# The first layer of a gated feed-forward block by seven products of halves, with its weights streamed from a scratch buffer in HBM

## The chip, the cores and the metric

The kernel runs on one core of a Trainium2 chip. The metric is the device time of one execution in microseconds (us); lower is better. A core has a matrix engine (PE in the profile; its weight loads have a row of their own, PEld), a vector engine (DVE), a scalar engine (ACT), a general engine (POOL), a queue processor that issues the transfers (SP), and 16 DMA engines between HBM and the on-chip memory SBUF. PE writes its results to eight PSUM banks of 128 x 512 float32, and DVE and ACT read them from there. Each engine works through its own instructions in the order in which they were written and waits on semaphores for the others.

## The reference

Eight batches with eight heads of attention: 512 local queries per head see 32 global keys and a window of 32 keys to each side; 32 global queries see everything. The 4608 rows that come out (512 features) go through a normalised, gated feed-forward block:

```python
rms = np.sqrt(np.mean(x * x, axis=-1, keepdims=True) + 1e-06)
xn = x / rms * rms_g
g = xn @ w_gate                         # 512 -> 1536
silu = g * (1.0 / (1.0 + np.exp(-g)))
val = xn @ w_val                        # 512 -> 1536
return (silu * val @ w_out).astype(np.float32)   # 1536 -> 512
```

## The kernel before

**Number format.** Every large product is done in float16 with operands split in a high and a low half: a product a*b is three matmuls, high*high, high*low and low*high, added up in float32 in PSUM. The weights are split and scaled on the chip at the start.

**Chunks.** The rows go through the block in nine chunks. Chunks 0 to 7 are the 512 local rows of one batch each; chunk 8 is the 256 global rows of all batches. Features lie on the partitions (four k-blocks of 128), rows on the free axis.

**First layer** (`moe_in`, L954 to L959, called by `moe_f`). The 1536 columns of each weight matrix are taken as 12 blocks f of 128. For each f and each of the two matrices (w = 0 gate, w = 1 value) 4 k-blocks x 3 matmuls of 128x128 weights by 512 rows add up in one PSUM bank, "pg" for the gate and "pv" for the value: 288 matmuls a chunk. Then ACT takes the tanh of the gate bank (L969), DVE makes the gated value from tanh and bank (L970) and multiplies it by the value bank (L977), ACT rounds to float16 (L980) and POOL takes the low half (L151, through the helper `sub`). All the split weights stay in SBUF, in 12 buffers "wf".

**Second layer** (`moe_block`, L1014). Four blocks of 128 rows, each 12 f x 3 matmuls of 512 columns into a "po" bank; ACT or DVE scales the result into SBUF (L1025, L1027) and SP stores it (L1028): 144 matmuls a chunk.

**Order.** Chunk 0 and the preparation of the weights follow a list written out by hand (`ORDER`); its letters name steps, for instance `N1`, `D1`, `U1`, `H1`, `Y1` for the norm of chunk 1 and `O`, `o` for the second layer of chunk 0. From chunk 1 on, each chunk is a list of 72 work items (48 of six first-layer matmuls, 24 of six second-layer matmuls). After each item `slot` issues those steps of the next chunk's attention that are due: loads L and V, scores S (L648), least value M and exponentials (L599, L610), division D (POOL, L625), turning T (DVE, L630), values A and B (L691), taking over X and Y (DVE, L704), and for the global queries GL, GS (L762), GM, GN, GT (L805), GA (L819), GD, GX. Each step has a least distance in items from the step that it needs. At items 56 to 66 the next chunk's norm follows, and `norm_split` (L946, L949, L149/L151) makes its four high and low operand tiles "xh" and "xl". Chunks 2 to 7 have two local attention units of four heads and, from gplan, one or two global units.

All transfers are issued on SP's queue, in order.

Of the kernel before, what the change touches and what calls it, by code (L numbers as in the profile page):

```python
# [22 lines left out]
P = 128  # L23
# [7 lines left out]
NGH = NG // 2  # L31
GC = 112
# [33 lines left out]
def attention_moe_kernel(  # L66
# [23 lines left out]
    LG = (4, 7)  # L90
# [6 lines left out]
    pool = ctx.enter_context(tc.tile_pool(name="pool", bufs=2))  # L97
    psum = ctx.enter_context(tc.tile_pool(name="psum", bufs=2, space=bass.MemoryType.PSUM))
# [92 lines left out]
    def gain_scale():  # L191
        power(gp[0], 1, 11, gs[:, 0:1])
# [114 lines left out]
    def group(g, fs):  # L307
# [22 lines left out]
        def powers():  # L330
            s = pool.tile([P, 2], F32, tag="ws", bufs=7, name=f"ws{g}")[:, :n]
            for j, f in enumerate(fs):
                scale[f] = s[:, j : j + 1]
            power(st["ps"], n, 15, s)
# [83 lines left out]
    job.update(K0=out_sum, K1=out_total, K2=out_scale)  # L418


    def local_unit(c, hp):
# [109 lines left out]
        def divide():  # L531
            assert len(xt) == hp
            xt.append(pool.tile([P, 512], F32, tag="x", bufs=4, name=f"x{c}_{hp}"))
# [31 lines left out]
    def local_halves(c, b, hp, xt):  # L565
# [25 lines left out]
        def softmax(x, bk, gs):  # L591
# [5 lines left out]
            for g in gs:  # L597
# [10 lines left out]
                )  # L608
            for g in gs:
# [90 lines left out]
        def take(z):  # L700
            x = pool.tile([P, 512], F32, tag="x", bufs=4, name=f"x{c}_{2 * hp + z}")
            xt.append(x)
            for half in range(2):
                nc.vector.tensor_copy(  # L704
                    x[:, half * 256 : (half + 1) * 256], st["a"][2 * z + half][:, :256]
                )
# [9 lines left out]
            ("S", scores, 1, [("L", LG[0]), ("^Y", 1)]),  # L716
        ]
        for j, (x, bk) in enumerate(((0, 0), (1, 0), (0, 1), (1, 1))):
            steps += [
                (f"M{j}", lambda x=x, bk=bk: softmax(x, bk, (0, 1)), 0, [("S", 2 * j + 1)]),  # L720
                (f"N{j}", lambda x=x, bk=bk: softmax(x, bk, (2, 3)), 0, [(f"M{j}", 1)]),
                (f"D{j}", lambda x=x, bk=bk: divide(x, bk), 0, [(f"N{j}", 2)]),
# [3 lines left out]
            ("A", lambda: values(blocks[:SPLIT]), 1, [("T3", 1), ("V", 4)]),  # L726
# [6 lines left out]
    def global_unit(b):  # L733
# [3 lines left out]
        def load():  # L737
# [5 lines left out]
            v = []  # L743
            for i in range(3):
                t = pool.tile([P, 1152], F32, tag="st", bufs=ST, name=f"gv{b}{i}")
                n = min(1024, 5 * 512 - i * 1024)
                nc.sync.dma_start(t[:GC, :n], gv[b, :, i * 1024 : i * 1024 + n])
                v += [t[:, j * 512 : (j + 1) * 512] for j in range(n // 512)]
            st.update(kq=kq, v=v)
# [88 lines left out]
        def turn():  # L838
# [8 lines left out]
            ("GS", scores, 1, [("GL", GG[0])]),  # L847
            ("GM", lambda: softmax(0), 0, [("GS", 1)]),
# [79 lines left out]
    def norm_all(ch, c, n):  # L928
# [3 lines left out]
        ps = attn_bank(f"ss{c}")  # L932
# [20 lines left out]


    def moe_in(ch, w, f, n, ps, ks):
        for k in ks:
            o = (w * NK + k) * P
            for i, (a, z) in enumerate(((0, "xh"), (0, "xl"), (1, "xh"))):
                nc.tensor.matmul(  # L959
                    ps[:, :n],  # L960
                    wf[f][:, a, o : o + P],
# [5 lines left out]
    def moe_gate(f, n, pg):  # L967
        t = pool.tile([P, 512], F32, tag="t", bufs=3, name=f"t{f}")
        nc.scalar.activation(t[:, :n], pg[:, :n], AF.Tanh, scale=half_inv[:, f : f + 1])  # L969
        nc.vector.scalar_tensor_tensor(t[:, :n], t[:, :n], 1.0, pg[:, :n], ALU.add, ALU.mult)  # L970
        return t

    def moe_h(ch, f, n, t, pv, on):
        if f % 2 == 0:
            ch["h"] = pool.tile([P, 2, 2, 512], F16, tag="h", bufs=NF // 2, name=f"h{f}")
        h = ch["h", f] = ch["h"][:, f % 2]
        nc.vector.scalar_tensor_tensor(  # L977
            t[:, :n], t[:, :n], c_h[:, f : f + 1], pv[:, :n], ALU.mult, ALU.mult
        )
        nc.scalar.copy(h[:, 0, :n], t[:, :n])  # L980
        sub(on, h[:, 1, :n], t[:, :n], h[:, 0, :n])

    def moe_f(ch, f, n, on):
        ps = {}

        def half(w, i):
            if i == 0:
                ps[w] = psum.tile(
                    [P, 512], F32, tag="pg" if w == 0 else "pv", bufs=1, name=f"p{w}_{f}"
                )  # L990
            moe_in(ch, w, f, n, ps[w], range(2 * i, 2 * i + 2))

        def gate():
            ps["t"] = moe_gate(f, n, ps[0])

        def inner():
            moe_h(ch, f, n, ps["t"], ps[1], on)
# [112 lines left out]
    for c in range(NCH):  # L1110
# [3 lines left out]
        for i, un in enumerate(units):  # L1114
# [6 lines left out]
            for name, fn, pe, after in steps:  # L1121
                st = {"name": name, "fn": fn, "pe": pe, "c": c, "x": xi, "after": [], "at": None}
                st["from"] = UNIT[len(units)][i]
# [16 lines left out]
    def ready(st):  # L1140
        if st["c"] > 0 and clock[0] < base.get(st["c"] - 1, 1 << 30) + st["from"]:
            return False
# [29 lines left out]
    first_chunk()  # L1172
    eng = mybir.EngineType
# [4 lines left out]
    assert not job, list(job)  # L1178
    row = SL
    for c in range(1, NCH):  # L1180
        n = width[c]
        ch = chunks[c]
        base.setdefault(c, clock[0])
        work = [w for f in range(NF) for w in moe_f(ch, f, n, "P")]
        work += [w for j in range(n // P) for w in moe_block(ch, j, row)]
        norm_at = NORM[0]
        last = c + 1 == B
        at = {}
        if c + 1 < NCH:
# [3 lines left out]
            at[NORM[1]] = lambda c=c, nx=nx: norm_sums(chunks[c + 1], c + 1, nx)  # L1193
            at[NORM[2]] = lambda c=c, nx=nx: norm_all(chunks[c + 1], c + 1, nx)
            at[NORM[3]] = lambda c=c, nx=nx: norm_split(chunks[c + 1], c + 1, nx)
        for k, (products, rest) in enumerate(work):
            products()
            if c + 1 < NCH:
                slot(1 if k < norm_at - 6 else 2, c + 1 if k < min(norm_at, SECOND) else c + 2)
                if k == norm_at - 1:  # L1200
                    while chunks[c + 1]["left"]:
                        slot(2, c + 1)
# [4 lines left out]
            if rest:  # L1207
                rest()
        row += n
# [126 lines left out]
```

## Time and profile before

| | |
|---|---|
| median of three runs | 981.94 us (979.61 to 983.16) |
| the profiled execution | 978.9 us, span of its instructions 977.1 us |
| PE, DVE, ACT, POOL busy | 939.2, 451.0, 409.2, 194.4 us |
| moved by the transfers issued in the kernel | 86.46 MB |
| one chunk of 512 rows in the steady part (280.89 to 389.62) | 108.73 us |

The span runs from the first to the last instruction; the 1.8 us between it and the profiled execution's own time lie around it. A busy PE is not a PE at its peak: matmuls are pipelined, each is shown with the time from its start to its end (379 ns for 512 columns) while the next starts 216 ns later. So the pace of a stretch of matmuls is read from its length and its count. In the groups by line a row gives the line, the engine, the operation, the names, the shapes and the count, then busy microseconds and the mean nanoseconds of one, then the idle time before it. The windows view gives one stretch in each row: its length, then for each engine the busy time and the count, the granted TensorE clock, the share of DMA time and the rate.

### The profile page before, as it was taken

Reading aid. Unit: us, or ns where it says so; the run is one execution under the profiler, and the core shown is the slowest. Engines: PE = TensorE matmul, PEld = TensorE weight load, DVE = VectorE, ACT = ScalarE, POOL = GpSimd, SP = SyncE. Lnnn points to the kernel's source line nnn. Section 1 sums busy time; section 2 is a strip of 40 time slices with the busy share of each in tenths; the row PEclk is TensorE's granted clock in tenths of the full one; section 3 lists DMA queues with packets and bytes.
Section 4 is the critical chain, followed back from the end, with each engine's and each line's share of the span. In section 5 each row is a group of like instructions: output and inputs, shape, how many; then the busy total and the mean of one; then the engine's idle time right before and its main releaser. Section 6 shows DMA issues by size and latency. Waiting matters only on the chain.

```text
span 977.1 us, 22949 instructions
## 1 busy us (share of the span) xinstructions
PE 939.2 (96%) x9732; PEld 486.3 (50%) x9732; DVE 451.0 (46%) x1369; ACT 409.2 (42%) x1070; POOL 194.4 (20%) x183
## 2 busy tenths in 40 slices
PE   6588999999999999999999999999999999999998
PEld 4444455445544544445444544455444544444584
DVE  6999973444244344434345244434334344232331
ACT  7999982434124341435124441435034431332131
POOL 0000000232213231223113140323114140111120
PEclk9799999999999999999999999999999999999999
DMA  9962421800044000710053001700062002400100
GB/s 355 406 261 93 152 88 38 269 31 2 23 167 116 16 2 33 254 32 1 23 188 110 2 12 44 233 31 2 23 212 85 2 13 82 142 1 1 40 5 22
DMA packets 31254, 88.24 MB, mean 90 GB/s; under 512 B 3632, under 2 KB 3888, under 8 KB 31152
## 3 DMA queue, kind: packets, MB, share of 16 engines
q1 hardware_dynamic: 30720, 86.46, 25.7%
q8 instruction: 76, 1.25, 0.5%
q10 hardware_dynamic: 432, 0.33, 0.1%
q14 instruction: 26, 0.21, 0.1%
HBM read 77.86 MB, written 8.91 MB: 89 GB/s over the span
## 4 chain that ended last, share of the span: by engine, by line
PE 86%; DVE 6%; DMA 5%; ACT 2%; issue 1%; SPq 0%; ACTq 0%; DVEq 0%
PE p L959 48%; PE po L1014 24%; PE a L691 3%; PE po L1081 3%; PE s L648 2%; DMA k<-in_qk_dram 2%; DMA v<-in_vw_dram 1%; DMA wr<-in_w_in_dram 1%; PE ga L819 1%; PE gt L805 1%; PE gs L762 1%; DVE wf L366 1%; ACT wr L265 1%; DMA gkq<-in_gkq_dram 1%; DVE t L1050 1%
## 5 line engine op out<-in xcount | busy, mean ns | idle before, releaser
L959 PE MATMUL p<-xh,wf 128*128 128x512 f16 (+1 forms) x1728 | 503.2, 368 | 8.3 <-DVE t L1050 6.3
L959 PEld LDWEIGHTS <-wf 128*128 128x128 f16 x2592 | 250.5, 98 | 280.1 <-issue 20.4
L959 PE MATMUL p<-xl,wf 128*128 128x512 f16 (+1 forms) x864 | 318.0, 368 | 0.0
L1014 PE MATMUL po<-wo,h 128*128 128x512 f16 x1080 | 237.4, 379 | 0.0
L151 POOL TENSOR_TENSOR h<-t,h 128x512 f16<-128x512 f32 (+1 forms) x96 | 105.2, 1095 | 565.9 <-ACT h L980 528.6
L1014 PEld LDWEIGHTS <-h 128*128 128x128 f16 x1080 | 104.8, 98 | 123.7
L970 DVE SCALAR_TENSOR_TENSOR t<-t,p 128x512 f32<-128x512 f32 (+1 forms) x96 | 62.8, 654 | 223.3 <-ACT t L969 223.3
L980 ACT CAST h<-t 128x512 f16<-128x512 f32 (+1 forms) x96 | 56.5, 588 | 164.8 <-DVE t L977 164.8
L969 ACT ACTIVATE t<-p,half_inv 128x512 f32<-128x512 f32 (+1 forms) x96 | 62.9, 656 | 115.8 <-PE p L959 100.5
L977 DVE SCALAR_TENSOR_TENSOR t<-t,c_h,p 128x512 f32<-128x512 f32 (+1 forms) x96 | 68.1, 710 | 78.6 <-PE p L959 78.6
L610 ACT ACTIVATE e<-e,sm 128x128 f32<-128x128 f32 x192 | 74.8, 390 | 40.6 <-DVE sm L599 40.6
L625 POOL TENSOR_TENSOR e<-e,sm 128x512 f32<-128x512 f32 x48 | 49.9, 1039 | 45.5 <-DVE sm L624 32.8
L1025 ACT ACTIVATE o<-po,kk 128x512 f32<-128x512 f32 x15 | 10.3, 688 | 114.2 <-PE po L1014 114.2
L599 DVE CUSTOM_DVE_ANT_0 e<-s,maskb 128x128 f32<-128x128 f32 x192 | 45.0, 281 | 5.6 <-PE s L648 5.6
L1027 DVE TENSOR_SCALAR o<-po,kk 128x512 f32<-128x512 f32 x15 | 11.3, 751 | 64.5 <-PE po L1014 64.5
L708 ACT ACTIVATE sq<-x 128x512 f32<-128x512 f32 x24 | 15.1, 628 | 55.7 <-DVE x L704 55.5
L630 DVE STREAM_TRANSPOSE et<-e 128x512 f32<-128x512 f32 x48 | 34.0, 708 | 7.5 <-POOL e L625 7.5
L691 PEld LDWEIGHTS a<-et,v 32*64 32x64 f32 x2112 | 31.0, 130 | 11.0 <-issue 10.2
L610 ACT ACTIVATION_READ_ACCUMULATOR e<-e,sm 128x1 f32 x192 | 35.8, 186 | 0.0
L691 PE MATMUL a<-et,v 32*64 32x96 f32 (+3 forms) x2112 | 35.5, 258 | 0.0
L704 DVE COPY x<-a 128x256 f32<-128x256 f32 x48 | 17.5, 416 | 38.2 <-PE a L691 38.2
L1081 PE MATMUL po<-wo,h 128*128 128x512 f16 x144 | 32.4, 379 | 0.0
(320 smaller groups left out, 743.5 us busy)
## 6 DMA issues: line engine op xcount, KB each, us to landing
wr<-in_w_in_dram SPq DMA_DIRECT2D x24, 512.0 KB, 10.0
k<-in_qkb_dram SPq DMA_DIRECT2D x24, 448.0 KB, 7.5
gkq<-in_gkq_dram SPq DMA_DIRECT2D x16, 576.0 KB, 8.0
out_dram<-o SPq DMA_DIRECT2D x34, 256.0 KB, 2.0
v<-in_vb_dram SPq DMA_DIRECT2D x24, 352.0 KB, 5.1
v<-in_vw_dram SPq DMA_DIRECT2D x16, 512.0 KB, 9.6
gv<-in_gv_dram SPq DMA_DIRECT2D x16, 448.0 KB, 10.9
wr<-in_w_out_dram SPq DMA_DIRECT2D x12, 512.0 KB, 4.1
```

The costliest lines, as they stand in the source:

```text
L151: nc.gpsimd.tensor_tensor(dst, a, b, ALU.subtract)
L599: nc.vector.tensor_tensor_reduce(out=e[:, g, :], in0=ps[:, g * P : (g + 1) * P], in1=late["mask"][:, m * P : (m + 1) * P], scale=-0.125, s ...
L610: nc.scalar.activation(e[:, g, :], e[:, g, :], AF.Exp, bias=sm[:, 0, j + g : j + g + 1], scale=-1.0, accum_out=sm[:, 1, j + g : j + g + 1],)
L625: nc.gpsimd.tensor_tensor(e, e, r.unsqueeze(2).to_broadcast([P, 4, P]), ALU.mult)
L691: nc.tensor.matmul(o, st["v"][x][r, m * D : (m + 1) * D], e, start=(m == blocks[0]), stop=(m == blocks[-1]), skip_group_check=True,)
L959: nc.tensor.matmul(ps[:, :n], wf[f][:, a, o : o + P], ch[z][k][:, :n], start=(k == 0 and i == 0), stop=(k == NK - 1 and i == 2),)
L969: nc.scalar.activation(t[:, :n], pg[:, :n], AF.Tanh, scale=half_inv[:, f : f + 1])
L970: nc.vector.scalar_tensor_tensor(t[:, :n], t[:, :n], 1.0, pg[:, :n], ALU.add, ALU.mult)
L977: nc.vector.scalar_tensor_tensor(t[:, :n], t[:, :n], c_h[:, f : f + 1], pv[:, :n], ALU.mult, ALU.mult)
L980: nc.scalar.copy(h[:, 0, :n], t[:, :n])
L1014: nc.tensor.matmul(ps[0], ch["h", f][:, a, j * P : (j + 1) * P], wo[f][:, z, :], start=(f == 0 and q == 0), stop=(f == NF - 1 and q == 2),)
L1081: nc.tensor.matmul(po[j], ch["h", f][:, a, j * P : (j + 1) * P], wo[f][:, z, :], start=(f == 0 and q == 0), stop=(f == NF - 1 and q == 2),)
```

## The change

**Seven products.** In chunks 2 to 7 the first layer is a product of a 2x2 block matrix, by Strassen's scheme in Winograd's form. The halves are: of the contraction, features 0 to 255 and 256 to 511; of the result, gate and value; of the rows, 0 to 255 and 256 to 511. `moe_pair` takes two f at a time (a pair, g = 0 to 5) and does the products in the order 6, 1, 5, 7, 2, 3, 4, each with 12 matmuls of 256 columns (2 f x 2 k x 3): 84 a pair, 504 a chunk. Products 7 and 4 add onto the bank of 6, 2 onto that of 1, 3 onto that of 5; 6, 1 and 5 are copied or summed into SBUF before the next product lands on their bank. So the gate u and the value v now stand in SBUF: ACT copies three banks a pair, DVE makes four sums of a bank and a tile, POOL one sum of two tiles. The two tanh, two gates, two inner products, two roundings and two low halves of a pair follow, spread over the next pair's first five products (`tail`).

**Operands.** `norm_halves` takes the place of `norm_split` for these chunks: four differences of halves on DVE, seven high halves on ACT, seven low halves on DVE (4) and POOL (3), at 7 to 17 items before the chunk's end.

**Weights.** `fold` makes, for each f, the four sums and differences of weight blocks (five instructions on DVE), their high half (ACT) and their low half (DVE), and writes them and the plain blocks to a scratch buffer in HBM: f = 0 to 2 in chunk 0 (J, j, u in `ORDER`), the rest in chunk 1, one f in 8 items. `fetch` reads them back: per pair three transfers of 512 KB and one of 256 KB, two pairs ahead, eight before chunk 2 and four a pair from there on; chunk 8 reads the plain blocks back. The 12 buffers "wf" hold the streamed tiles and the sums u, v, s of the pairs.

**Order.** A chunk 2 to 7 has 66 items (42 of 12 matmuls, 24 of six). Attention may now start up to 26 items before its chunk's turn, exponentials are steps of their own, half of "take" goes from DVE to ACT, the global unit loads two of its value tiles later, the norm comes 22 to 17 items before the end; the norm's small PSUM result uses "pg". In `moe_f` (chunks 1 and 8) the banks alternate between "po" and "pg"/"pv", and gate, rounding and low half come one or two items later.

The diff, cut to what the text speaks of:

```diff
-S6 C5.0 ... Q7 O2.2 Z7 O2.3 N1.0 ... N1.12 D1 O3.2 O3.3 ...
+... Q7 O2.2 Z7 J0 j0 u0 O2.3 N1.0 ... N1.12 D1 J1 j1 u1 J2 j2 u2 O3.2 O3.3 ...
-    NORM = (56, 59, 61, 66)
-    UNIT = {2: (0, 20), 3: (2, 19, 33)}
+    NORM = {1: (16, 15, 13, 11)}
+    NORMS = (22, 21, 19, 17)
+    FIRST = (0, 19, 31)
+    UNIT = {2: (0, 20), 3: (-26, 2, 12)}
+    FOLD = 8
...
+    def fold(f):
...
+        def sums():
...
+            nc.vector.tensor_tensor(t[0], wf[f][:, 0, :], wf[f][:, 1, :], ALU.add)
+            nc.vector.tensor_tensor(s[:, 1], a[:, 2], a[:, 3], ALU.add)
+            nc.vector.tensor_tensor(s[:, 0], s[:, 1], a[:, 0], ALU.subtract)
+            nc.vector.tensor_tensor(s[:, 2], a[:, 0], a[:, 2], ALU.subtract)
+            nc.vector.tensor_tensor(s[:, 3], a[:, 1], s[:, 0], ALU.subtract)
...
+    def fetch(c, g, i):
+        t = pool.tile([P, 2, 2, 2, HT], F16, tag="wf", bufs=NF, name=f"wt{c}_{g}{i}")
+        ops = [(0, 2 * i, 2)] if i < 3 else [(0, 6, 1)]
...
+    def moe_pair(ch, g):
+        bank = {6: "po", 1: "pg", 5: "pv"}
+        onto = {7: 6, 4: 6, 3: 5, 2: 1}
...
+            for j in range(2):
+                for k in range(2):
+                    for i, x in ((0, hi), (0, lo), (1, hi)):
+                        nc.tensor.matmul(
+                            ps[:, j * HT : (j + 1) * HT],
+                            w[:, j, i, k * P : (k + 1) * P],
+                            x[:, k * HT : (k + 1) * HT],
...
+        def rest(p):
...
+            if p == 6:
...
+                nc.scalar.copy(s(6), st["ps", 6])
+            elif p == 1:
...
+                nc.scalar.copy(s(1), st["ps", 1])
+            elif p == 5:
+                nc.vector.tensor_tensor(s(5), st["ps", 5], s(1), ALU.add)
+                nc.gpsimd.tensor_tensor(s(6), s(6), s(1), ALU.add)
+            elif p == 7:
+                put("v", 7, s(5), 1)
+            elif p == 2:
+                put("u", 2, None, 0)
+            elif p == 3:
+                put("u", 3, s(6), 1)
+            else:
...
+                    nc.scalar.activation(
+                        t, st["u"][:, j, :], AF.Tanh, scale=half_inv[:, f : f + 1]
+                    )
+                put("v", 4, s(1), 0)
...
+        def gate(j):
+            t, u = st["t", j], st["u"][:, j, :]
+            nc.vector.scalar_tensor_tensor(t, t, 1.0, u, ALU.add, ALU.mult)
...
+        if EARLY <= c < B:
+            work = [w for g in range(NF // 2) for w in moe_pair(ch, g)]
+        else:
+            work = [w for f in range(NF) for w in moe_f(ch, f, n, "P")]
```

More of the change, by code (lines that the diff above doesn't have):

```diff
@@ L418, in attention_moe_kernel, with x_part @@
     job.update(K0=out_sum, K1=out_total, K2=out_scale)
+    def x_part(c, hp):
+        ch = chunks[c]
+        if hp % 2 == 0:
+            ch["xx", hp // 2] = pool.tile([P, 2, 512], F32, tag="x", bufs=2, name=f"x{c}_{hp}")
+        return ch["xx", hp // 2][:, hp % 2, :]
     def local_unit(c, hp):
@@ L700, in take @@
         def take(z):
-            x = pool.tile([P, 512], F32, tag="x", bufs=4, name=f"x{c}_{2 * hp + z}")
+            x = x_part(c, 2 * hp + z)
             xt.append(x)
[L703 to L706, printed above, removed]
+            nc.scalar.copy(x[:, :256], st["a"][2 * z][:, :256])
+            nc.vector.tensor_copy(x[:, 256:], st["a"][2 * z + 1][:, :256])
             sq = pool.tile([P, 512], F32, tag="w", bufs=3, name=f"sq{u}{z}")
@@ L742, in load, with load_v @@
                 kq += [t[:, :576], t[:, 576:]]
[L743 to L749, printed above, removed]
+            st.update(kq=kq, v=[])
+            load_v(0)
+        def load_v(i):
+            t = pool.tile([P, 1152], F32, tag="st", bufs=ST, name=f"gv{b}{i}")
+            n = min(1024, 5 * 512 - i * 1024)
+            nc.sync.dma_start(t[:GC, :n], gv[b, :, i * 1024 : i * 1024 + n])
+            st["v"] += [t[:, j * 512 : (j + 1) * 512] for j in range(n // 512)]
         def scores():
@@ L957, in moe_in @@
             o = (w * NK + k) * P
+            if "wt" in ch:
+                q, o = k // 2 if w == 0 else 1 - k // 2, k % 2 * P
+                rows = ch["wt"][f // 2, w][:, q, f % 2]
+            else:
+                rows = wf[f]
             for i, (a, z) in enumerate(((0, "xh"), (0, "xl"), (1, "xh"))):
@@ L960, in moe_in @@
                     ps[:, :n],
-                    wf[f][:, a, o : o + P],
+                    rows[:, a, o : o + P],
                     ch[z][k][:, :n],
@@ L965, in moe_in, with later @@
                 )
[L967 to L981, printed above, removed]
+    pend = {}
+    def later(slots, fn):
+        pend.setdefault(tick[0] + slots, []).append(fn)
+    tick = [0]
     def moe_f(ch, f, n, on):
@@ L1140, in ready @@
     def ready(st):
-        if st["c"] > 0 and clock[0] < base.get(st["c"] - 1, 1 << 30) + st["from"]:
+        if clock[0] < base.get(st["c"] - 1, 1 << 30) + st["from"]:
             return False
@@ L1172, in attention_moe_kernel @@
     first_chunk()
+    folds = {f: fold(f) for f in range(NF)}
+    for f, steps in folds.items():
+        for n, fn in zip("Jjuw", steps):
+            job[f"{n}{f}"] = fn
     eng = mybir.EngineType
@@ L1177, in attention_moe_kernel, with feed @@
         job.pop(name)()
-    assert not job, list(job)
+    stores = [steps[3] for f, steps in folds.items() if f"J{f}" not in job]
+    folds = {f: steps for f, steps in folds.items() if f"J{f}" in job}
     row = SL
+    left = list(folds.values())
+    ring = [(c, g, i) for c in range(EARLY, B) for g in range(NF // 2) for i in range(4)]
+    ring += [(B, g, i) for g in range(NF // 2) for i in range(2)]
+    def feed():
+        if ring:
+            fetch(*ring.pop(0))
+    base[1] = 0
     for c in range(1, NCH):
@@ L1192, in attention_moe_kernel @@
                 at[norm_at] = lambda: norm(chunks[B], B, nx)
-            at[NORM[1]] = lambda c=c, nx=nx: norm_sums(chunks[c + 1], c + 1, nx)
-            at[NORM[2]] = lambda c=c, nx=nx: norm_all(chunks[c + 1], c + 1, nx)
-            at[NORM[3]] = lambda c=c, nx=nx: norm_split(chunks[c + 1], c + 1, nx)
+            for i, fn in enumerate((norm_sums, norm_all, norm_split)[: 3 if last else 2]):
+                at[total - gaps[i + 1]] = lambda c=c, nx=nx, fn=fn: fn(chunks[c + 1], c + 1, nx)
+            if not last:
+                for i, fns in norm_halves(chunks[c + 1], c + 1).items():
+                    at[total - gaps[3] + i] = lambda fns=fns: [fn() for fn in fns]
         for k, (products, rest) in enumerate(work):
@@ L1208, in attention_moe_kernel @@
                 rest()
+            for fn in pend.pop(tick[0], []):
+                fn()
+            tick[0] += 1
+            if EARLY <= c < B and k >= 7 and k % 7 < 5 and k <= first + 4:
+                ch["tail", k // 7 - 1][k % 7]()
+            if c == 1:
+                if k == 1:
+                    for fn in stores:
+                        fn()
+                for i, steps in enumerate(left):
+                    for d, step in zip((0, 2, 3, 5), steps):
+                        if k == FOLD * i + d:
+                            step()
+                if -12 <= k - total < -4:
+                    feed()
+            elif c < B and k < first and k % 7 in (1, 3, 5, 6):
+                feed()
+            elif c == B - 1 and first <= k < first + 8:
+                feed()
         row += n
```

250 lines of the change are left out of this document (210 added, 40 removed).

## The prediction

> **What bounds the kernel now.** I read the page first, then the windows by chunk, then the chain of waits inside one steady chunk.
>
> ```profile
> span 977.1 us, 22949 instructions
> PE 939.2 (96%) x9732; PEld 486.3 (50%) x9732; DVE 451.0 (46%) x1369; ACT 409.2 (42%) x1070; POOL 194.4 (20%) x183
> ```
> ```profile
> 0.00:44.00 44.00, 22.41 (x634) 17.61 (x634) 33.34 (x149) 35.92 (x102) 0.20 (x4) 0.83 0.98 377
> ...
> 170.70:280.89 110.19, 108.15 (x1166) 53.59 (x1165) 45.84 (x146) 39.53 (x116) 28.09 (x25) 1.00 0.23 75
> 280.89:389.62 108.73, 108.08 (x1167) 53.54 (x1165) 45.23 (x145) 38.84 (x115) 28.10 (x25) 1.00 0.22 73
> ...
> 824.56:926.17 101.61, 101.51 (x682) 48.19 (x681) 29.11 (x67) 26.27 (x52) 17.62 (x17) 1.00 0.18 57
> ```
>
> The columns after the length are PE, PEld, DVE, ACT, POOL, then clock, DMA share and GB/s. From 171 us on PE is never free: 108.08 of 108.73 us in chunk 2, at full granted clock, with DVE, ACT and POOL under half and DMA at 0.22. So a chunk lasts as long as its matmuls, and only fewer or shorter matmuls make it shorter.
>
> ```profile
> 317.37 0.02 issue
> 317.39 0.75 DVE t L977
> 318.14 0.34 DVE x L704
> 318.49 0.14 issue
> 318.62 1.02 PE gs L762 x16
> ...
> 342.43 13.06 PE p L959 x60
> ...
> 376.67 12.96 PE po L1014 x60
> ```
>
> That is the chain of chunk 2. It is PE's own matmuls but for one wait, 317.37 to 318.62 = 1.25 us, where the scores of the global unit wait for DVE to free their banks. The 60 uninterrupted matmuls of 512 columns give the pace: 12.96 / 60 = 0.216 us each.
>
> **The matmuls.** Removed: 288 of 512 columns a chunk, 288 x 0.216 = 62.2 us. Added: 504 of 256 columns, each with a weight load of its own. The trace holds this very instruction: chunk 8 has 256 rows and its first layer is 288 such pairs of load and matmul, without interruption.
>
> ```profile
> 926.17 31.44 PE p L959 x288
> ```
> ```profile
> 926.17:957.61 31.44, 31.44 (x288) 27.93 (x286) 1.00 0.03 10
> ```
>
> 31.44 / 288 = 0.1092 us. The second row (PE, PEld, clock, DMA share, GB/s) shows that the 27.93 us of loads lie inside the 31.44 us of matmuls. So 504 x 0.1092 = 55.0 us, and a chunk loses 62.2 - 55.0 = 7.2 us of PE time; six chunks (2 to 7) lose 43.2 us. The ideal of seven eighths would be 7.8 us a chunk; a product then takes 12 x 0.1092 = 1.31 us and a pair 9.17 us instead of 62.2 / 6 = 10.37 us. Second layer, attention and chunk 8 keep their matmuls. [...]
>
> **The banks.** Before, each bank was emptied at the end of an f. Now a bank must be read within two products, 2 x 1.31 = 2.62 us, before the third lands on it.
>
> ```profile
> L970 DVE SCALAR_TENSOR_TENSOR t<-t,p 128x512 f32<-128x512 f32 x84 | 57.7, 687 | 207.0 <-ACT t L969 207.0
> L149 DVE TENSOR_TENSOR xl<-x,xh 128x512 f16<-128x512 f32 x12 | 16.8, 1436 | 6.0 <-ACT xh L949 6.0
> L149 DVE TENSOR_TENSOR h<-t,h 128x512 f16<-128x512 f32 x12 | 8.2, 683 | 0.0
> L704 DVE COPY x<-a 128x256 f32<-128x256 f32 x48 | 17.5, 416 | 38.2 <-PE a L691 38.2
> L630 DVE STREAM_TRANSPOSE et<-e 128x512 f32<-128x512 f32 x48 | 34.0, 708 | 7.5 <-POOL e L625 7.5
> ...
> L366 DVE SCALAR_TENSOR_TENSOR wf<-w1t,ws,wf 128x1024 f16<-128x1024 f32 x1 | 1.3, 1279 | 0.0
> ```
> ```profile
> L514 ACT COPY pt<-t 128x512 f32<-128x512 f32 x16 | 8.7, 580 | 2.9 <-PE a L523 2.5 <-PE t L509 0.4
> ...
> L363 ACT ACTIVATE wf<-w5t,ws 128x1024 f16<-128x1024 f32 x1 | 1.2, 1170 | 0.0
> ```
> ```profile
> L151 POOL TENSOR_TENSOR h<-t,h 128x512 f16<-128x512 f32 x84 | 97.1, 1156 | 536.0 <-ACT h L980 498.6 <-DVE sm L599 37.4
> L625 POOL TENSOR_TENSOR e<-e,sm 128x512 f32<-128x512 f32 x48 | 49.9, 1039 | 45.5 <-DVE sm L624 32.8 <-ACT e L610 12.8
> ```
> ```profile
> 280.89:355.49 74.60, 73.95 (x845) 36.90 (x843) 31.11 (x115) 33.64 (x106) 21.05 (x19) 1.00 0.30 94
> 355.49:389.62 34.13, 34.13 (x323) 16.64 (x322) 14.12 (x31) 5.20 (x9) 7.04 (x6) 1.00 0.07 25
> ```
>
> The last two rows are the first and the second layer of chunk 2, with that chunk's share of attention. A pair adds four sums on DVE (4 x 0.687), three copies on ACT (3 x 0.580) and a sum on POOL (1.04). In the first layer, now 74.6 - 7.2 = 67.4 us, DVE has 31.1 + 24 x 0.687 = 47.6 us (71%), ACT 33.6 + 18 x 0.58 = 44.0 us, POOL 21.1 + 6.2 = 27.3 us (40%). No engine replaces PE as the bound. A sum of 0.687 us leaves 2.62 - 0.69 = 1.93 us of spare; ahead of it in DVE's queue can stand an attention step of an earlier item (a turn 0.708) and a gate or inner product, about 0.7 each: one or two fit, three do not. So there will be waits now and then. Both ends: nothing, since in the old order gate banks were refilled one value product (12 x 0.216 = 2.59 us) after their last matmul, with tanh and L970 in between, and the waits of PE name no L969 to L977; or one such instruction a pair, 0.69 x 36 = 25 us. I take 1.0 us a chunk, nearer the lower end by those rows: 6 us. The old wait of 1.25 us I leave as it is; its lower end is that it vanishes in all six chunks (7.5 us gained).
>
> **Two SBUF inputs.** Gate and inner product now read u and v from SBUF, not PSUM. In the rows above the same subtraction takes DVE 0.683 us alone and 1.436 us where POOL subtracts at the same time (L149). With POOL busy 40% of the stage, 24 such instructions a chunk cost some 24 x 0.4 x 0.75 = 7 us of DVE, 55 of 67 us in all: still hidden. [...]
>
> **Operands and second layer.** `norm_halves` adds four differences, and four low halves replace two: 4 x 0.683 + 4 x 0.683 - 2 x 1.436 = 2.6 us of DVE, three casts of ACT. It stands 17 to 7 items before the chunk's end, beside second-layer matmuls, where DVE has 14.12 of 34.13 us: hidden. If that cover were gone, the next chunk's first product would wait at most those 2.6 us. The last pair's tail runs under the first second-layer block: its f = 10, 11 are needed after 30 matmuls = 6.5 us, and sum, two gates, two inner products, rounding and low half are 5 x 0.69 + 0.6 + 0.7 = 4.7 us: no wait.
>
> **Folding the weights.** One f costs DVE 1.279 + 4 x 0.416 + 1.279 = 4.2 us, ACT 1.17 us.
>
> ```profile
> 152.91 0.88 DVE L868 TENSOR_SCALAR dg<-ident,rn 128x128 f32<-128x128 f32 x4
> 164.58 0.75 DVE L1094 TENSOR_SCALAR o<-po,kk 128x512 f32<-128x512 f32 x1 [10.80 <-PE po L1081]
> ```
>
> In chunk 0 DVE is idle for 10.8 us here. Three folds take 12.6 us, one of them ahead of the norm of chunk 1, so results and low operands of chunk 1 may come up to 1.8 us late. In chunk 1 nine folds add 38 us: 45.8 + 38 = 84 of 110 us of DVE. Gates there have two items more than before since the banks alternate, but scores and turns can stand behind a block of 1.279 + 4 x 0.416 = 2.9 us. Between nothing and two such blocks (5.9 us) I take 1.5 us in all, for DVE's free time is nearest to covering it.
>
> **The stream.** A product's weights are 128 x 2 x 2 x 256 x 2 B = 256 KB, so 1.8 MB a pair, 11.0 MB a chunk.
>
> ```profile
> q1 hardware_dynamic: 30720, 86.46, 25.7%
> wr<-in_w_in_dram SPq DMA_DIRECT2D x24, 512.0 KB, 10.0
> k<-in_qkb_dram SPq DMA_DIRECT2D x24, 448.0 KB, 7.5
> ```
>
> Writing 12.6 MB and reading six times 11.0 and once 6.3 MB doubles the 86.46 MB. In the first layer 94 x 74.6 / 67.4 + 11.0 MB / 67.4 us = 267 GB/s, under the 377 that the first 44 us moved at share 0.98. A transfer is issued 13 products (17 us) ahead of its use, and 512 KB landed in 10.0 us with the queues full. SP gets 24 issues more a chunk; a fetch can stand behind a store that waits for its result, yet stores wait only in the second layer, where no fetch is due. Cost: nothing; if the lead is used up, the rival below.
>
> **The sum.** 43.2 - 6 - 1.5 = 35.7 us. The profiled execution, 978.9 us, becomes 943.2. It lies 3 us under the median of the three runs, 981.94 us; the same difference gives 946 us.
>
> **The rivals.** (1) The other engines answer late: each pair loses one DVE instruction, 25 us instead of 6. Gain 43.2 - 25 - 1.5 = 17 us, 965 us. For it: DVE above 70% in strict order, with attention in the same queue. Against: 1.93 us of spare. (2) Slower: the gate and inner product lose against POOL. If each of the 24 waits out a whole POOL instruction, 1.156 us, DVE has 47.6 + 27.7 = 75.3 us in a stage that used to last 74.6, so each chunk is 0.7 us longer than before: 6 x 0.7 + 6 + 1.5 = 12 us, 994 us. It decides from (74.6 - 47.6) / 24 = 1.13 us each; the measured 0.75 us stays under. (3) The stream runs dry. With 13 products of lead a pair lasts 7/13 of a landing; break-even is 10.37 us, a landing of 19.3 us. At 20 us: 36 x (10.77 - 10.37) + 1.5 = 16 us, 998 us. Against: 10.0 us at a full queue. (4) Loads do not hide, so a matmul of 256 columns costs 0.109 + 0.097 (27.93 / 288) = 0.206 us: 504 x 0.206 = 104 us, 42 us more a chunk, 1233 us. [...]
>
> **How the numbers follow.** Forecast 0.65, rival 1 0.20, rival 2 0.07, rival 3 0.04, rival 4 0.01; 0.03 that losses just eat the gain. Within 0.5% (4.9 us, about what a measurement of this kernel can tell from no change): 0.03; faster 0.85; slower 0.12. The range runs from 935 (no new waits and some of the old 1.25 us gone) to 966 (rival 1).
>
> **What would show it.** Chunks 2 to 6 should last 108.7 - 6.2 = 102.5 us, with 84 matmuls of a pair in 9.2 us where no attention lies between, DVE near 64 us a chunk, PE's waits on DVE or ACT about 1 us a chunk. Chunk 1 should stay at 110 to 112 us. The prediction is wrong if matmuls of 256 columns start more than 0.115 us apart, if PE waits over 3 us a chunk, above all for L149-like sums, gates or wf transfers, or if chunk 1 grows by over 5 us.

## The result, and the profile after

The changed kernel takes 949.26 us (948.95 to 949.54, four runs) beside 981.8 us before, a ratio of 0.967 (0.965 to 0.969). The profiled execution went from 978.9 to 949.54 us; here the two differ by 29.4 us, 3 us less than the medians, since the profiled execution of before lay under its median.

The page's first lines, the span and the busy time of each engine:

```profile
span 947.5 us, 26480 instructions
...
PE 900.5 (95%) x11028; PEld 615.5 (65%) x11028; DVE 635.3 (67%) x1603; ACT 496.2 (52%) x1232; POOL 254.2 (27%) x219
...
q1 hardware_dynamic: 73824, 171.41, 54.8%
```

PE has 39 us less work by the profile's count, DVE 184 us more, and the bytes moved have doubled. Where the time went is read from the windows by chunk. Rows: chunk 1; the start of chunk 2 up to the global unit's scores; chunks 3, 4 and 5. Columns: length, then PE, PEld, DVE, ACT, POOL, clock, DMA share, GB/s.

```profile
170.91:289.83 118.92, 113.66 (x1295) 57.08 (x1293) 86.19 (x225) 52.80 (x153) 32.60 (x26) 0.97 0.66 204
289.83:310.83 21.00, 16.55 (x269) 12.49 (x274) 11.85 (x26) 9.44 (x23) 7.76 (x6) 0.76 0.89 285
400.21:502.19 101.98, 100.24 (x1386) 74.38 (x1383) 67.90 (x172) 51.53 (x140) 37.48 (x31) 1.00 0.57 186
502.19:602.88 100.69, 100.19 (x1383) 74.32 (x1383) 67.89 (x172) 51.59 (x140) 37.46 (x31) 1.00 0.58 188
602.88:702.89 100.01, 100.01 (x1382) 74.30 (x1383) 67.89 (x172) 51.53 (x140) 37.47 (x31) 1.00 0.58 189
```

A steady chunk went from 108.73 to 102.0, 100.7 and 100.0 us (chunks 3 to 5); in the last PE is never free. The forecast was 102.5 us. Chunk 1 went from 110.19 to 118.92 us; 2.0 us of that are scores of chunk 3 that the new order does there. And the start of chunk 2 runs at a granted clock of 0.76 and takes 21.0 us. Where nothing is folded (below) chunk 2 does the same in 14.0 us; chunk 3, which has less attention there, takes 10.7 (400.21 to its scores at 410.90).

What PE waited for, in all, first from 300 us on and then from 168 to 312 us (columns: total, times, longest):

```profile
PE pq L1108 <- issue: 2.2, 2, 1.7
PE gs L780 <- DMA gkq<-in_gkq_dram: 1.7, 1, 1.7
PE po L1266 <- POOL h L157: 0.5, 1, 0.5
```
```profile
PE s L664 <- DMA k<-in_qkb_dram: 3.3, 2, 2.0
PE a L707 <- DVE et L646: 2.3, 1, 2.3
PE pq L1108 <- DVE ht L155: 2.1, 1, 2.1
PE a L707 <- issue: 1.9, 1, 1.9
```

In 647 us of seven products PE waited 4.4 us, and never for a bank that another engine had still to read. In the 144 us around the folding it waited 9.6 us. The chain of waits in chunk 5 shows the pace of the new first layer:

```profile
637.57 22.38 PE pq L1108 x204
659.95 1.47 PE a L707 x64
661.42 2.73 PE pq L1108 x24
```

22.38 / 204 = 0.1097 us a matmul, so 504 of them take 55.3 us.

### The profile page after: what moved, and what is told of

Read it like the earlier page. It is cut to its first block, busy times and chain, and to the rows that moved or that the text cites. A ratio compares the mean times of both kernels' runs of the same rounds, so it can differ in the third digit from the quotient of the medians.

```text
span 947.5 us, 26480 instructions
## 1 busy us (share of the span) xinstructions
PE 900.5 (95%) x11028; PEld 615.5 (65%) x11028; DVE 635.3 (67%) x1603; ACT 496.2 (52%) x1232; POOL 254.2 (27%) x219
## 4 chain that ended last, share of the span: by engine, by line
PE 80%; DMA 8%; DVE 7%; ACT 2%; issue 1%; SPq 1%; POOL 0%; ACTq 0%; DVEq 0%; POOLq 0%
PE pq L1108 35%; PE po L1266 22%; PE p L1205 9%; PE a L707 4%; PE po L1333 3%; PE s L664 3%; DMA k<-in_qk_dram 2%; DMA k<-in_qkb_dram 1%; DMA v<-in_vw_dram 1%; DMA wr<-in_w_in_dram 1%; DMA wt<-wd 1%; PE gs L780 1%; PE ga L837 1%; DMA gkq<-in_gkq_dram 1%; PE gt L823 1%
## 5 line engine op out<-in xcount | busy, mean ns | idle before, releaser
L1108 PEld LDWEIGHTS <-wt 128*128 128x128 f16 x3024 | 293.5, 98 | 46.0 <-issue 8.7
L1108 PE MATMUL pq<-xh,wt 128*128 128x256 f16 x1152 | 204.0, 274 | 0.5 <-issue 0.5
L157 POOL TENSOR_TENSOR h<-t,h 128x512 f16<-128x512 f32 (+1 forms) x90 | 101.7, 1135 | 280.2 <-ACT h L1248 244.8
L1108 PE MATMUL pq<-ht,wt 128*128 128x256 f16 x1296 | 157.0, 273 | 3.9 <-DVE ht L155 2.1
L1108 PE MATMUL pq<-xl,wt 128*128 128x256 f16 x576 | 157.9, 274 | 0.0
L1205 PE MATMUL p<-xh,wf 128*128 128x512 f16 x384 | 120.4, 386 | 6.9 <-DVE t L1302 6.6
L1205 PEld LDWEIGHTS <-wf 128*128 128x128 f16 x576 | 56.2, 99 | 75.7 <-issue 14.4
L1140 POOL TENSOR_TENSOR s<-s,s 128x512 f32<-128x512 f32 x36 | 48.6, 1350 | 190.7 <-ACT s L1137 115.1
L1162 DVE SCALAR_TENSOR_TENSOR t<-t,c_h,v 128x512 f32<-128x512 f32 x72 | 74.5, 1042 | 0.0
L1205 PE MATMUL p<-xl,wf 128*128 128x512 f16 x192 | 73.9, 385 | 0.0
L1126 DVE TENSOR_TENSOR v<-pq,s 128x512 f32<-128x512 f32 x72 | 49.6, 689 | 31.1 <-PE pq L1108 30.5
```

What stands on the lines that cost most here:

```text
L157: nc.gpsimd.tensor_tensor(dst, a, b, ALU.subtract)
L1108: nc.tensor.matmul(ps[:, j * HT : (j + 1) * HT], w[:, j, i, k * P : (k + 1) * P], x[:, k * HT : (k + 1) * HT], start=first, stop=(p in end ...
L1126: nc.vector.tensor_tensor(o, ps, x.rearrange("p (j n) -> p j n", j=2), ALU.add)
L1140: nc.gpsimd.tensor_tensor(s(6), s(6), s(1), ALU.add)
L1162: nc.vector.scalar_tensor_tensor(t, t, c_h[:, f : f + 1], st["v"][:, j, :], ALU.mult, ALU.mult)
L1205: nc.tensor.matmul(ps[:, :n], rows[:, a, o : o + P], ch[z][k][:, :n], start=(k == 0 and i == 0), stop=(k == NK - 1 and i == 2),)
```

## The experiments

Theory V says that the loss around chunk 1 comes from DVE's time for the folding, theory T from the transfers of its stores. All differences below are to 949.3 us, the changed kernel's median; a repeat on another chip gave 951.7 us (below), so 2 us between such medians mean little.

**No folding at all.** `sums`, `high`, `low` and `store` do nothing, and `fetch` reads a given array:

```diff
+    wd = [given[g].rearrange("p (o j a n) -> p o j a n", o=8, j=2, a=2) for g in range(NF // 2)]
...
-            nc.vector.tensor_tensor(t[0], wf[f][:, 0, :], wf[f][:, 1, :], ALU.add)
...
+            pass
```

> Leaves out the folding of the weights altogether: no sums, no high and low halves, no stores; the seven products stream given float16 numbers of the same layout from HBM, so the result is not the reference's. Theory V (the gain of the changed kernel is cut by folding in chunk 1, through DVE's time): chunk 1 and the start of chunk 2 lose their 15.5 us, so 949.3 - 15.5 = 934 us (931 to 937). Rival T (cut by the transfers of the stores): the same 934 us, since both are gone. Rival O (chunk 1 is longer because of the new order of its attention and banks, not because of the folding): 945 to 949 us.

Measured: 936.9 us (934.9 to 938.1). The folding costs 12.3 us; O falls. Its chunk 1 and start of chunk 2:

```profile
171.31:283.24 111.93, 109.78 (x1296) 54.98 (x1294) 52.38 (x183) 47.09 (x154) 30.48 (x27) 1.00 0.36 116
283.24:297.26 14.02, 12.88 (x269) 10.70 (x273) 6.99 (x11) 6.36 (x14) 6.74 (x5) 1.00 0.85 285
```

So the loss has two halves: 118.92 - 111.93 = 7.0 us in chunk 1 and 21.00 - 14.02 = 7.0 us at the start of chunk 2. The two spans differ by less than these 14.0 us, 947.5 - 936.1 = 11.4 us: in the run without folding chunk 3 is 1.8 us longer (103.8 for 102.0). Of that a longer wait of PE (2.0 us for 1.7 on "issue") accounts for 0.3 us; the rest is not explained.

**The sums alone, the stores alone.** In the first of these `store` does nothing and `fetch` reads the given array; in the second the sums go and `store` writes plain blocks:

```diff
-            for q, o, n in ((0, 0, 1), (1, 2, 2), (3, 5, 1)):
-                nc.sync.dma_start(to[:, o : o + n], st["d"][:, q : q + n])
+            for q, o, n in ((0, 0, 1), (1, 2, 2), (3, 5, 1)):
+                own = wf[f].rearrange("p a (q n) -> p q a n", q=4)
+                for i in range(n):
+                    nc.sync.dma_start(to[:, o + i], own[:, q + i])
```

> Keeps the sums and halves on DVE and ACT, leaves out the seven stores of each f and streams given numbers (not the reference's result). Theory V: DVE and ACT are as full as before, so most of the loss stays: 945 to 949 us. Rival T: the waits for keys, for code and for the queue go, 934 to 938 us. Rival O: 945 to 949 us, with the first run there too.

> Leaves out the sums and halves on DVE and ACT; the stores write plain blocks of the weights in their place, the same bytes in eight transfers of 128 KB an f (not the reference's result). Theory V: 935 to 938 us, only the keys' late landing of 3.3 us may stay. Rival T: 945 to 949 us. Rival O: 945 to 949 us.

Measured: 947.8 us (943.8 to 948.6) with the sums alone, 945.4 us (943.3 to 948.0) with the stores alone. Each theory met its range in one run and missed it in the other: each half alone leaves most of the loss, and the two do not add up. The windows tell them apart better than the medians. Sums alone, then stores alone, chunk 1 and the start of chunk 2 of each (the last row runs on to the last of the scores' waits):

```profile
170.86:285.84 114.98, 111.97 (x1296) 56.55 (x1293) 86.37 (x225) 52.73 (x153) 32.62 (x26) 0.99 0.34 114
285.84:305.71 19.87, 14.59 (x269) 11.54 (x274) 11.86 (x26) 9.43 (x23) 7.77 (x6) 0.91 0.73 230
```
```profile
170.69:288.69 118.00, 113.20 (x1296) 56.76 (x1293) 52.37 (x183) 47.09 (x154) 30.45 (x27) 0.97 0.67 200
288.69:305.90 17.21, 13.54 (x270) 10.82 (x268) 7.68 (x12) 7.21 (x15) 7.07 (x5) 1.00 1.04 331
```

In chunk 1 the stores alone cost 118.00 - 111.93 = 6.1 us and the sums alone 3.1 us of the 7.0. At the start of chunk 2 the sums alone cost 19.87 - 14.02 = 5.9 us; the stores alone 3.2 us, of which 2.5 us are the scores' wait for their keys. So V holds for most of the start of chunk 2, T for most of chunk 1. Each row is one execution; in a second profile of the changed kernel the same two stretches are up to 1.5 us shorter, so the shares are rough:

```profile
171.75:289.18 117.43, 112.29 (x1296) 56.90 (x1294) 86.33 (x225) 52.82 (x153) 32.62 (x26) 0.99 0.67 207
289.18:309.14 19.96, 14.69 (x269) 11.53 (x273) 11.85 (x26) 9.43 (x23) 7.77 (x6) 0.91 0.92 298
```

**The folds earlier.**

```diff
-    FOLD = 8
+    FOLD = 6
```

> One f folded every 6 items instead of 8: the last two folds leave the end of chunk 1, where the operands of chunk 2 are made. Theory V: the 8.8 us at the start of chunk 2 mostly go, while DVE is fuller in the first 53 items and gives some back: 941 to 946 us. Rival T: the same bytes in a shorter time, 949 to 953 us. Rival O: no change, 948 to 950 us.

Measured: 950.7 us (948.9 to 952.9), inside T's range and no clear change. The windows show why:

```profile
170.81:294.22 123.41, 113.37 (x1295) 55.99 (x1293) 91.16 (x239) 55.56 (x163) 33.59 (x27) 0.99 0.68 211
294.22:308.17 13.95, 12.81 (x261) 10.65 (x259) 6.99 (x11) 6.29 (x14) 6.66 (x5) 1.00 0.87 271
```

The start of chunk 2 is free of loss (13.95 us), as V has it, but chunk 1 is 4.5 us longer: there PE now waits 4.7 us for keys (3.3 before) and 3.3 us for turns (none before). That V was right about one place did not make its sum right.

**The first unit's scores later.**

```diff
-            ("S", scores, 1, [("L", LG[0] if c == EARLY else LG[1]), ("^Y", 1)]),
+            ("S", scores, 1, [("L", LG[1] if c > EARLY else 6 if hp == 0 else LG[0]), ("^Y", 1)]),
...
-    FIRST = (0, 19, 31)
+    FIRST = (0, 21, 31)
```

> Only the order of chunk 1's attention changes: the first unit's scores stand two items later behind their loads, the global unit two items later. Theory W (PE's first wait in chunk 1, 3.3 us for keys that land 6.6 us after their issue, is a matter of where the scores stand): that wait goes and nothing replaces it, 946 us (945 to 947). Rival M (it moves on: DVE and the queue behind are late anyway): 948 to 950 us.

Measured: 948.4 us (947.0 to 952.7), inside the scatter. In its profile PE's wait for the keys falls from 3.3 to 1.2 us, but others grow: all its waits from 168 to 312 us sum to 9.5 us, for 9.6 in the changed kernel. That is M.

**The low half on POOL.** The edit before, and:

```diff
-    FOLD = 8
+    FOLD = 7
...
-            sub("V", st["d"][:, :, 1, :], st["s"], st["d"][:, :, 0, :])
+            sub("P", st["d"][:, :, 1, :], st["s"], st["d"][:, :, 0, :])
```

> As the run before, and the low half of the folded sums goes from DVE to POOL and one f is folded every 7 items. Theory V (DVE is too full at the start of chunk 2): DVE loses 9 x 1.2 us in chunk 1, the last fold ends before the operands of chunk 2 are made, the 7 us lost there mostly go: 938 to 942 us. Rival P (POOL's two-input instructions of some 2.3 us hold DVE's two-input ones up as long): 944 to 949 us.

Measured: 945.2 us (942.3 to 949.4), in P's range and above V's. It was run once more beside the changed kernel (below); the windows stand there.

**More work for DVE in a pair.** To see how far the banks' spare reaches, `put("v", 7, s(5), 1)` was done twice, then four times:

```diff
             elif p == 7:
                 put("v", 7, s(5), 1)
+                for _ in range(3):
+                    put("v", 7, s(5), 1)
```

> Each pair writes the upper half of v twice: one more DVE instruction of 0.69 us a pair, 36 in all, the bank of products 6, 7 and 4 is read 0.69 us longer. Theory S (the banks' spare of 1.9 us hides it): 949 to 951 us. Rival L (the other engines are at their limit): PE waits for each, up to 36 x 0.69 = 25 us, 960 to 974 us.

> The same with three more writes, 2.07 us a pair. Theory S: the four together hold the bank 4 x 0.69 = 2.76 us and a little to start, more than the two products of 2.62 us that follow, so now each pair waits 0.2 to 0.7 us, 7 to 25 us in all: 956 to 974 us. Rival L: 3 x 25 us more, over 1000 us.

Measured: 950.7 us (950.3 to 951.7) with one more, 972.9 us (969.9 to 975.5) with three more. The first 25 us of DVE work are free, as S has it; of the 74 us of three, 23.7 us show. The chain of waits with three more, where one pair waits:

```profile
616.24 2.74 PE pq L1108 x24
...
619.00 0.70 DVE v L1126
...
621.18 0.70 DVE v L1126
621.88 0.04 issue
621.92 1.47 PE pq L1108 x12
```
```profile
PE pq L1108 <- DVE v L1126: 19.1, 27, 1.2
```

Four writes take 621.88 - 619.00 = 2.88 us from the end of product 7 to the start of product 4; the products 2 and 3 between hide 2.6 us of a free queue, and what stands ahead in the queue adds to the wait: 27 waits, 19.1 us.

**Two queues, and the changed kernel again.** The edits of the POOL run, and the plain blocks' stores on ACT's queue:

```diff
-                nc.sync.dma_start(to[:, o], wf[f][:, :, q * HT : (q + 1) * HT])
+                nc.scalar.dma_start(to[:, o], wf[f][:, :, q * HT : (q + 1) * HT])
```

> As the run with the low half on POOL; the four stores of plain blocks of each f go to ACT's queue, the three of sums stay on SP's. Theory Q (part of what is left of the loss is that loads stand behind stores in SP's queue): keys and the global unit's values land earlier, 941 to 944 us. Rival R (it is the 16 DMA engines that are full, the queue does not matter, and ACT now spends time on issuing): 945 to 949 us.

> The changed kernel unaltered, as the measure for the others on this chip: 949 us (948 to 951) by every theory.

> The run with the low half on POOL once more, beside the changed kernel on one chip: 945 us (943 to 947), 3 to 5 us under the changed kernel, if that difference was more than the scatter of its runs; otherwise the two lie within 2 us.

Measured: 954.7 us (953.4 to 958.5) with two queues; the changed kernel 951.7 us (950.7 to 953.1), 2 us above its first runs; the low half on POOL 944.0 us (943.2 to 948.0). With two queues the time is above both ranges. Q falls: the keys landed no earlier (5.7 us after their issue at the median between 165 and 312 us, 5.0 in the changed kernel), and the issues hold up ACT's own work.

```profile
ACT wq L1065 <- DMA wd<-wf: 15.1, 1, 15.1
```

From 173.9 to 189.0 us ACT did nothing but work through twelve such issues, which waited for earlier stores, and casts and tanh stood behind them. The low half on POOL is the fastest of the kernels that do the whole work: a ratio to the kernel before of 0.962 (0.960 to 0.965) beside 0.969 (0.967 to 0.972) for the changed kernel on the same chip, 7.7 us. Its windows show chunk 1 at 117.24 and the start of chunk 2 at 15.48 us, with a wait of the scores of 1.2 us at the end of it:

```profile
170.62:287.86 117.24, 111.57 (x1295) 55.73 (x1293) 82.43 (x228) 55.26 (x161) 52.18 (x37) 1.00 0.68 212
287.86:303.34 15.48, 13.48 (x269) 10.78 (x267) 8.29 (x14) 7.13 (x17) 6.60 (x5) 1.00 0.90 301
```

Up to the first of the scores (301.50) that start takes 13.6 us, no more than without folding, so what V said of this place came true. Chunk 1 stays 5.3 us longer than without folding. This kernel has three edits at once (the scores' place, the folds' spacing, the low half on POOL); only the first was also run alone.

**The kernel before, its global unit two items later.**

```diff
-    UNIT = {2: (0, 20), 3: (2, 19, 33)}
+    UNIT = {2: (0, 20), 3: (2, 21, 33)}
```

> The kernel before the change with its global unit two items later. Theory G (the steady chunks gain more than 7.2 us because the old wait of 1.25 us a chunk was one of order): this wait of PE goes in six chunks, 982 - 7 = 975 us (974 to 977). Rival H (the scores wait for banks that are freed no earlier, or another wait takes its place): 981 to 983 us.

Measured: 975.3 us (972.3 to 977.3), ratio 0.993 (0.990 to 0.995). The old wait was one of order: G holds. So 6.7 of the change's 32.5 us could be had without the seven products. Its steady chunk lasts 107.54 us, 1.2 less than before, and PE is never free in it:

```profile
285.46:393.00 107.54, 107.54 (x1167) 53.49 (x1166) 45.42 (x145) 38.62 (x115) 28.09 (x25) 1.00 0.22 73
```

Chunk 5 of the changed kernel has the same attention, so what the seven products alone gave is 107.54 - 100.01 = 7.5 us a chunk.

## Why the prediction was right, point by point

The forecast of 946 us was 3 us off. That is in part luck: the steady part came out 6 us better than forecast, the folding 12 us worse. In the profiled executions 35.7 us were forecast and 29.4 us came.

**The matmuls: right.** The forecast pace from chunk 8 was 0.1092 us, measured 0.1097, so 55.3 us a chunk for 55.0; by the lengths of whole chunks the saving was 7.5 us for 7.2. The streamed tiles kept the pace of the resident ones to half a percent; rival 4 falls, as 57.14 us of weight loads lie inside a first layer of 65.23 us, attention included (chunk 5):

```profile
602.88:668.11 65.23, 65.23 (x1028) 57.14 (x1029) 40.36 (x96) 36.06 (x90) 26.01 (x22) 1.00 0.77 244
668.11:702.89 34.78, 34.78 (x356) 17.16 (x354) 27.53 (x76) 15.47 (x51) 11.46 (x9) 1.00 0.23 87
```

**The banks: right in kind, the size at the lower end.** The forecast took 6 us of new waits; there are none of this kind. The spare of 1.93 us was real: one more instruction of 0.69 us a pair cost nothing, three more cost 23.7 us. Rival 1 falls. In the first layer DVE is at 40.4 of 65.2 us (62%, forecast 71%), because the new order has moved part of the attention into the second layer, where DVE has 27.5 of 34.8 us.

**The old wait: wrong.** The sum left it as it is; that it vanishes (7.5 us) stood only as one end. It went, and the run with the global unit later shows that order alone removes it, for 6.7 us. With the banks this made the steady part some 6 us better than forecast.

**Two SBUF inputs: right that it stays hidden.**

```profile
L1162 DVE SCALAR_TENSOR_TENSOR t<-t,c_h,v 128x512 f32<-128x512 f32 x12 | 12.5, 1048 | 0.0
...
L1158 DVE SCALAR_TENSOR_TENSOR t<-t,u 128x512 f32<-128x512 f32 x12 | 7.8, 680 | 0.0
```

The 12 inner products of chunk 5 take 1.048 us in the mean, where the one from PSUM took 0.742; the gates 0.680, no more than before. That is 12 x 0.306 = 3.7 us a chunk for the 7 us forecast. The mean mixes two kinds: in the timeline eight take 0.74 us, and four take 1.6 to 1.8 us, those during which POOL works on a low half (L157, three of them) or a sum of squares (L724). So the price of one meeting, some 0.9 us (the mean of the four less 0.74), was above the 0.75 us taken, but only 4 of the 24 paid it and not 40%. Rival 2 would need 1.13 us on each of the 24.

**Operands and the last pair: hidden but for two places.** No wait for the operands was forecast, 2.6 us at most if their cover were gone. PE waits for them once, 2.1 us at the start of chunk 2, where the folding had filled DVE. The tail of the last pair makes PE wait 0.5 us once, for a low half that POOL took 1.13 us for where 0.7 was taken.

**The folding: the step that failed, by its size.** 1.5 us were taken and 12.3 us measured (14.0 us in the profiles: 7.0 in chunk 1, 7.0 at the start of chunk 2). Two things went wrong. DVE's free time was counted over the whole of chunk 1 (84 of 110 us; measured 86 of 119), while the loss sits where the last two folds, the operands of chunk 2 and the turns for chunk 3 meet; there DVE has 4.90 and 5.00 of 5 us:

```profile
285.00:290.00 5.00, 5.00 (x25) 2.25 (x23) 4.90 (x8) 1.75 (x5) 0.23 (x1) 1.00 1.02 329
290.00:295.00 5.00, 2.84 (x14) 1.35 (x12) 5.00 (x17) 4.24 (x13) 1.37 (x2) 0.81 0.96 323
295.00:300.00 5.00, 2.71 (x80) 2.26 (x81) 3.84 (x5) 1.63 (x4) 4.20 (x3) 0.50 0.84 274
300.00:305.00 5.00, 5.00 (x96) 3.73 (x95) 0.66 (x1) 0.58 (x1) 1.26 (x1) 0.67 0.94 295
```

And the stores were priced at nothing, by a mean rate, though by the stores-alone run they are most of the 7.0 us in chunk 1. The prediction's bound of 5.9 us was too narrow for the same reason. Its own sign of being wrong came true here: chunk 1 grew by 8.7 us, 6.7 without the scores that moved into it, where over 5 was the sign. And the loss is paid twice. Against the run without folding PE waits 3.1 us more in chunk 1 (5.2 for 2.1) and 3.3 us more at the start of chunk 2 (4.4 for 1.1). The other 7.6 of the 14.0 us are for the most part matmuls at half clock behind these waits: PE is busy for 14.0 us at a granted clock of 0.50 in the two stretches, which at twice the usual spacing (last section) costs an estimated 7.0 us; without folding the clock is 1.00 in both. The prediction did not have this at all (last section).

**The stream: right for reading.** 512 KB landed in 4.7 us (median), no wait of PE names the transfer of a product's weights, and rival 3 falls. What the transfers did cost stands under the folding.

**The sum.** Steady part 37.2 us forecast, 43.5 measured (before 280.89 to 977.1 is 696.2 us, after 289.83 to 947.5 is 657.7; the difference 38.5, plus the 7.0 lost at its start, less 2.0 for the scores moved into chunk 1). Folding 1.5 forecast, 7.0 + 118.92 - 110.19 - 2.0 = 13.7 measured. 43.5 - 13.7 = 29.8, the spans differ by 29.6.

## What to carry to other kernels

Price a matmul of another width from a stretch of the same kernel that already has it; that gave the pace of the new matmuls to within half a percent. Count the spare of each engine in the few microseconds where new work lands, not over a stage, and give bulk stores a price of their own even when their mean rate is low. A one-time preparation for a saving that repeats six times can cost close to a third of it; look at it as closely as at the loop. And price a wait of PE of some 2 us higher than its length: here matmuls at half clock followed several waits of 1.9 us and more, though not all of them.

## What the runs showed of the hardware that was not expected

**Half clock followed some short waits of PE.** In the changed kernel, PE waits 1.86 us at 208.51; from 211.2 to 214.6 us its matmuls start 0.43 us apart instead of 0.216. Rows: the stretch with this wait and the one behind it; the stretch with the wait of 2.1 us at the start of chunk 2 and the one behind it, which holds the wait of 2.3 us; and from the kernel with the low half on POOL three stretches around a wait of 2.29 us (181.83 to 184.12):

```profile
207.77:211.18 3.41, 1.55 (x75) 1.13 (x66) 1.73 (x3) 1.52 (x3) 1.42 (x1) 1.00 0.67 201
211.18:214.59 3.41, 3.41 (x10) 1.21 (x8) 0.96 (x2) 0.95 (x2) 0.00 (x0) 0.50 0.99 258
289.69:293.11 3.42, 1.29 (x12) 0.90 (x11) 3.42 (x15) 2.38 (x7) 1.04 (x1) 1.00 0.95 326
293.11:303.35 10.24, 7.92 (x103) 5.17 (x101) 5.73 (x8) 4.07 (x11) 4.77 (x4) 0.50 0.89 277
```
```profile
179.09:182.51 3.42, 2.75 (x132) 1.94 (x130) 1.20 (x5) 1.12 (x5) 0.40 (x1) 1.00 1.09 351
182.51:185.92 3.41, 1.80 (x9) 0.86 (x10) 0.29 (x1) 0.00 (x0) 0.00 (x0) 1.00 0.99 302
185.92:189.33 3.41, 3.41 (x18) 1.52 (x17) 3.27 (x5) 0.62 (x1) 1.42 (x1) 1.00 0.76 228
```

The half clock lasts 3.41 us in the first case and 10.24 us in the second. A third stretch of 3.41 us, from 180.47 us, begins in the second of two waits for keys, 2.0 and 1.3 us long. Behind the waits of 1.7 us that end at 436.93 and 838.72 us there is none: the clock is 1.00 in the mean from 310.83 us to the end. Other runs show both as well. With the stores alone PE waits 2.7 us between 200 and 210 us, and from 210 to 220 us the clock is 0.83. The kernel before with its global unit later waits 4.4 us between 180 and 190 us, where the clock is 0.76, and 0.90 in the 10 us behind. But with the low half on POOL the clock stays at 1.00 in all three rows around the wait of 2.29 us, and behind a second wait of 2.29 us, which ends at 430.02 us, 203 matmuls take 22.33 us, 0.110 us each. So the length of a wait alone does not settle it; what does is not shown.

**PE waits for nothing that the profile names.** The changed kernel has a wait of 1.9 us on "issue" in chunk 1, with a DMA share of 0.88 between 200 and 210 us; stores alone had 2.7 us, sums alone none there, no folding 0.5 us. The kernel before, which stores no weights, had 1.4 us, and with its global unit later 4.4 us, with a DMA share of 1.04 between 180 and 190 us.

What the traces show at these waits is a packet on the queue q8, which the page calls "instruction". The pages count 76 such packets for the 19464 matmuls and weight loads of the kernel before, and 86 for 22056 in the changed one: one packet for about 256 of them in both. After 165 us these two traces have four waits of PE on "issue" of over 0.3 us, 1.39 us to 183.14 in the kernel before and 1.86, 1.74 and 0.50 us to 210.37, 436.93 and 540.01 in the changed one. All four end 1.4 to 1.6 us after the end of such a packet, though in the changed kernel the packets come 9 us apart at the median; the packet for the wait to 210.37 ends at 208.76. Before each of the four PE had started 141 to 163 matmuls in 5 us, mostly short ones of attention, where the changed kernel starts 46 at the median. So these waits came behind dense stretches of short matmuls. That PE waited for its own next instructions is the author's reading of this; no run shows it. Whether other transfers hold the packets up is not shown either: the wait to 436.93 came with a DMA share of 0.59 (433 to 437 us).
